# Threshold attention and a SwiGLU block on one core: the first nested output product issued in two pieces, with the last group's fourth product between them

## The chip, the core and the metric

The kernel runs on one core of a Trainium2 chip. A core has TensorE (PE: matmuls, and beside them its weight loads, PEld), VectorE (DVE), ScalarE (ACT), GpSimd (POOL) and SyncE (SP), which here issues DMA transfers. The metric is device time in microseconds (us) of one execution; lower is better. Before the change three runs took 1370.97, 1372.1 and 1374.73 us; the median is 1372.1 us.

## The reference

Attention in which only scores near the row's maximum survive, then a gated feed-forward block on the result:

```python
scores = scale * q @ k.T                      # per batch (8) and head (8), 576 x 576, head size 64
thresh = max(scores) - tau
scores = where(scores >= thresh, scores, -1e9)
attn   = softmax(scores)                      # with 1e-9 added to the sum
x      = concat_heads(attn @ v)               # 4608 tokens x 512
g      = x @ w_gate                           # 512 x 1536
out    = (g * sigmoid(g) * (x @ w_val)) @ w_out   # 1536 x 512
```

All numbers are float32.

## The kernel before

**Blocks.** The tokens are worked off in blocks 0 to 8. Blocks 0 to 7 hold the first 512 tokens of a batch each, as two halves t = 0, 1 of 256 tokens; block 8 holds the remaining 64 tokens of all batches. While the attention of one batch runs, the feed-forward part of the block before it is woven in. One block takes 12 slots of the attention loop; a slot (`slot_scores`, line 1705; `slot_rest`) is one set of score matmuls (tile names `sc`), their row maxima on VectorE, exponentials on ScalarE (line 1751), masking on VectorE (line 1753), scaling (line 1779 on ScalarE, line 1776 on POOL) and transposes (line 1781). In every third slot `attend` (line 1802, tiles `xa`) multiplies finished attention rows with v. It takes two PSUM banks, and ScalarE copies its result out (lines 1813, 1814).

**Gates and values.** The first feed-forward product and the value product of a block are made in six groups g (class `Group`), each with seven smaller matmul products instead of eight: p1 to p7, all through `mul` (line 993, tiles `pa`, `pb`, `pe`). The fourth product, `p4` (line 1073), adds the last part to bank `pb`. Its method `finish` (line 1041) then has ScalarE take the tanh of the gate (line 1045), VectorE multiply it with the bank's content (line 1046, output in `hall`), and POOL multiply by the halved gate (line 846). p4 needs the copy that ScalarE makes of the bank after p7 (line 1068). `gates_and_values` issues p4 of a group after p1 of the next one; for the last group there is no next one, and `end_gates` issues it from the output part.

**Output products.** For blocks 2 to 8 class `Deep` (line 1399) makes the product with `w_out` from seven half-size products, as a block matrix with two by two parts: a11, a12 (first half of the tokens), a21, a22 (second half), and sums of them. Five of the seven operands are split once more: `nested` (line 1462) issues seven sub-products of three 128 x 128 x 128 matmuls each (line 1473, tiles `px`), into two PSUM banks. Their operands come from `inner_sums` (line 1446): four sums j3, j1, j2, j4 of quarters of the operand, each 384 wide, on POOL in blocks 2 to 6 and on VectorE in the last two. The order of the sub-products in a nested product is

```python
ORDER = 0, 1, 3, 6, 4, 5, 2
```

where 0, 1 and 3 read quarters of the operand as it is, and 6, 4, 5 and 2 read the sums j3, j1, j2 and j4. Two of the seven operands stay whole (`flat`, line 1482, tiles `py`).

The steps of a block of `Deep` are, in blocks 2 to 6: `p1` (first nested product, operand a11, then ScalarE's copies of its two banks, lines 1495 and 1496), `gates_end` (the last group's p4, then `late`), `p2` (second nested product, operand a12, added in the same banks), `p5` (flat), `p6` (nested), `p3` (flat), `p7` and `p4` (nested). `p1` and `gates_end` come in slot 9 of the block, `p2` and `p5` in slot 10, `p6` and `p3` in slot 11, `p7` and `p4` in slots 0 and 1 of the next. Slot 10 begins with `attend` and the next scores, so between `gates_end` and `p2` TensorE runs xa and sc.

`late` (line 1431) plans the sums for the second product into the place of a11, so they wait for the first product, which reads a11:

```python
self.inner_sums(1, self.a12, self.a11, self.ready["a12"], self.m1, *j3)
```

then the sums a21 + a22 and a22 - s3, and last the sums of the operand of `p6` in the place where the sums for the first product were.

**Order.** A planner (`Plan`, line 31) runs along TensorE's order as it is written. For every job of another engine it keeps an estimated duration, the jobs it depends on and a rank; it issues the open jobs of each engine by estimated start and rank. An engine then executes its instructions in the order in which they were issued.

Of the kernel before, what the change touches and what calls it, by code (L numbers as in the profile page):

```python
# [27 lines left out]
class Plan:  # L28
# [68 lines left out]
    def pe(self, took, fn, *deps):  # L97
        self.force(*deps)
        for d in deps:
            if d is not None:  # L100
                self.t = max(self.t, (d.end if isinstance(d, Job) else d) + self.HOP)
        self.run(self.t)
        fn()
        self.t += took
        return self.t + self.PIPE
# [7 lines left out]
def kernel(  # L113
# [32 lines left out]
    NF2, DM2 = NF // 2, DM // 2  # L146
# [35 lines left out]
    NQ = 7  # L182
# [343 lines left out]
    def attend_tile(copy=lambda xa, fn: (fn(), give_back(xa))):  # L526
        if not unattended:
            return
        if not xts:
            for u, lo in enumerate((0, 2 * XW)):  # L530
                xts["full", u] = xall[:, lo:lo + XW].rearrange("p (c n) -> p c n", c=NCC)
            xts["last", 0] = xlast
        seg, t, pT, pT2 = unattended.popleft()
        vr, vr2 = seg["v"]
        n = pT2.shape[1]
        xa = bank("xa")
        for kt in range(KT):
            for h in range(2):
                nc.tensor.matmul(xa[h * D:(h + 1) * D, 0:n], vr[:, h, kt, :], pT[:, h, kt, :],
                                 start=(kt == 0), stop=False)  # L540
        nc.tensor.matmul(xa[:, 0:n], vr2, pT2, start=False, stop=True)
        u, lo = divmod(t * P, TC)
        to = xts[("last", 0) if t == NT else ("full", u)][:, seg["i"], lo:lo + n]
        copy(xa, lambda: nc.scalar.copy(to, xa[:, 0:n]))
# [155 lines left out]
    for n, seg in enumerate(segs[:2 * NP]):  # L700
# [3 lines left out]
        for x, t in enumerate(seg["tiles"]):  # L704
# [47 lines left out]
            if later and (n == NP or n == NP - 1 and x == 0):  # L752
                to, fr = later.popleft()
# [218 lines left out]
    tail = [False]  # L972
    MM = 0.4325
    gated = {}

    class Group:
# [25 lines left out]
        def p1(self, early=True):  # L1002
            self.a = take("pa")
            self.m1 = self.mul(self.a, self.w[0], x_block(self.c, 0, 0), True, *self.w_deps[0], *self.a.deps, *ready_x[self.c][0])
            self.a.bank.full = True
            if early:
                self.take_b()
# [10 lines left out]
        def p2(self):  # L1018
            u, self.u1_old = turn_of(u_bufs)
            self.u1_buf = u  # L1020
            if self.b is None:
                self.s1 = job("ACT", 0.55, lambda: nc.scalar.copy(u.ap, self.a.rows()), self.m1, *self.u1_old, rank=0)
                self.u1_old = []
            m = self.mul(self.a, self.w[1], x_block(self.c, 0, 1), False, *self.w_deps[1], self.cb if self.b else self.s1)
            self.m2 = m
# [70 lines left out]
    def four_sums(places, a11, a12, a21, a22, *deps):  # L1096

        p1, p2, p3, p4 = places
        j1 = job("DVE", 0.36, dve_tt(p1, a21, a22, ALU.add), *deps, rank=1)
        j2 = job("DVE", 0.36, dve_tt(p2, p1, a11, ALU.subtract), j1, rank=1)  # L1100
        j4 = job("DVE", 0.36, dve_tt(p4, a12, p2, ALU.subtract), j2, rank=1)
        return [j4, job("DVE", 0.36, dve_tt(p3, a11, a21, ALU.subtract), j4, rank=1)]
# [42 lines left out]
    class LateGroup(Group):  # L1145
        def nested(self, o, first, *deps):
            begun = set() if first else {0, 1}
            sums, wd = late_sums[self.c, self.g]
            ready, xd = x_deep[self.c]

            def fn():
                for n in ORDER:
                    b_, at_ = AT[n]
                    nc.tensor.matmul(self.es[b_].ap()[:, at_ * P:(at_ + 1) * P], wd[o][n], xd[o][n], start=b_ not in begun, stop=True,  # L1154
                                     skip_group_check=True)
                    begun.add(b_)

            return pe(NQ * MM / 2, fn, *deps, *sums, *ready)
# [231 lines left out]
    def weights_of(o):  # L1390
        b11, t3, b21, b22 = quarters(operands[o])
        return (b11, b21, b22, deeper_part(o, 2), deeper_part(o, 0), deeper_part(o, 1), t3)
# [3 lines left out]
    CW = NQ * P  # L1396
    spaces = tall[:, 0:CW], tall[:, CW:2 * CW], vall[:, NJ * D:NJ * D + CW]

    class Deep:


# [28 lines left out]

        def late(self, mark):
            c, n = self.c, NF2 // 2
            self.ready["a12"] = [gated[c, 0, n + x] for x in range(n)]
            self.ready["a22"] = [gated[c, 1, n + x] for x in range(n)]
            j3 = self.ready["s3"]
            self.inner_sums(1, self.a12, self.a11, self.ready["a12"], self.m1, *j3)
            self.ready["s1"].append(self.sum(self.a21, self.a21, self.a22, ALU.add, n - 1, j3[n - 1], gated[c, 1, NF2 - 1], rank=1))
            self.ready["s2"] = [self.sum(self.s2, self.a22, self.s3, ALU.subtract, x, j3[x], gated[c, 1, n + x], mark, rank=1) for x in range(n)]
            self.inner_sums(5, self.s2, self.place, self.ready["s2"], self.m1)

        def sum(self, out, a, b, op, x, *deps, rank=2):
            fs = slice(2 * x, 2 * x + 2)
# [16 lines left out]
        ORDER = 0, 1, 3, 6, 4, 5, 2  # L1459
        AT = {0: (0, 0), 1: (0, 1), 5: (0, 2), 2: (0, 3), 3: (1, 0), 4: (1, 1), 6: (1, 2)}  # L1460

        def nested(self, o, holds, first, *deps):

            ws = weights_of(o)
            begun = set() if first else {0, 1}
            for n in self.ORDER:
                a, ready = self.inner[o][n]
                bank_, at_ = self.AT[n]

                def fn(n=n, a=a, bank_=bank_, at_=at_):  # L1470
                    ps = holds[bank_].ap()[:, at_ * P:(at_ + 1) * P]
                    for f in range(NF2 // 2):
                        nc.tensor.matmul(ps, a[:, f, :], ws[n][:, f, :], start=bank_ not in begun, stop=True, skip_group_check=True)  # L1473
                        begun.add(bank_)

                m = pe(0.67, fn, *ready, *deps, *deep_jobs[o])
            return m
# [76 lines left out]

        def p1(self):
            self.x, deps = self.pair("px")
            self.m1 = self.nested(0, self.x, True, *deps)
            self.c1 = self.copies(self.spaces[0], self.x, self.m1, *u_list[0].jobs, *u_list[1].jobs)

        def gates_end(self):  # L1560
            end_gates()
            self.late(plan.t + plan.PIPE)

        def p2(self):
            m = self.nested(1, self.x, False, *self.c1)
# [322 lines left out]
    def end_gates():  # L1888
        state.pop("last_product")()
# [64 lines left out]
    for s, (n, x) in enumerate((n, x) for n in range(len(halved)) for x in range(NU3)):  # L1954
# [13 lines left out]
        elif s == 1:  # L1968
            box = []
            m = pe(1.0, lambda: attend_tile(lambda *y: box.extend(y)))  # L1970
# [93 lines left out]
```

## Time and profile before

| what | us |
|---|---|
| median of three runs | 1372.1 |
| lowest, highest run | 1370.97, 1374.73 |
| span of the profiled execution | 1369.2 |
| median run less that span | 2.9 |
| TensorE matmuls busy | 1351.0 |
| VectorE, ScalarE, POOL busy | 1070.9, 875.5, 719.9 |

The profile is of one execution, taken apart from the three runs. Its own time is its span, from the first to the last instruction, and what lies around it; the page gives no separate run time for it, so the distance to the median of the runs is shown instead. Times in the views are us from the span's start. In the chain of waits a row is start, length, engine, tile, line and how many records; each matmul appears as two records. `LNNN` is a line of the kernel.

### The profile page before, as it was taken

How to read it: one execution, taken by the hardware profiler on the slowest of the kernel's cores; microseconds unless marked ns; L12 is line 12 of the kernel's file. 1: busy time of each engine (PE TensorE's matmuls, PEld its weight loads, DVE VectorE, ACT ScalarE, POOL GpSimd, SP SyncE). 2: the span in 40 equal slices, each digit the busy share in tenths (PEclk: the TensorE clock that was granted, in tenths of full speed). 3: DMA queues.
4: the chain of work that ended last, by engine and by line, in shares of the span. 5: the costliest groups of instructions: out<-in, count | busy, mean ns of one | idle time of the engine just before them, and what ended most of it. 6: DMA issues, size and time to landing. Idle time of an engine off the chain costs nothing.

```text
span 1369.2 us, 39187 instructions
## 1 busy us (share of the span) xinstructions
PE 1351.0 (99%) x15590; PEld 1116.1 (82%) x15590; DVE 1070.9 (78%) x2815; ACT 875.5 (64%) x2277; POOL 719.9 (53%) x665
## 2 busy tenths in 40 slices
PE   8999999999999999999999999999999999999998
PEld 7777787778788788877887888877887788999998
DVE  7878888887887777777778777777777776787786
ACT  6888776666756766677776766776767764330330
POOL 2688598663564669434973387427943593000000
PEclk9999999999999999999999999999999999999999
DMA  8752424545525540654154513553165403524411
GB/s 177 200 185 90 82 60 133 146 121 156 151 52 155 144 98 27 181 159 117 37 171 128 150 36 128 144 144 87 36 192 144 113 19 143 162 78 146 151 66 32
DMA packets 208294, 162.32 MB, mean 119 GB/s; under 512 B 166128, under 2 KB 180464, under 8 KB 202736
## 3 DMA queue, kind: packets, MB, share of 16 engines
q1 hardware_dynamic: 203920, 158.86, 41.3%
q8 instruction: 124, 2.03, 0.6%
q10 hardware_dynamic: 4192, 0.95, 0.3%
q14 instruction: 58, 0.48, 0.1%
HBM read 138.28 MB, written 21.50 MB: 117 GB/s over the span
## 4 chain that ended last, share of the span: by engine, by line
PE 90%; DVE 3%; DMA 2%; POOL 2%; SPq 1%; issue 1%; ACT 1%; ACTq 0%; DVEq 0%; POOLq 0%
PE pb L993 18%; PE pa L993 12%; PE px L1473 12%; PE sc L1705 10%; PE pe L993 9%; PE xa L1802 9%; PE po L1269 5%; PE py L1482 5%; PE sc L1154 2%; PE pg L1200 2%; PE pv L1200 2%; PE pe L1154 1%; SPq L367 1%; DMA wo<-in_moe_w_val_dram 1%; PE sc L1473 1%
## 5 line engine op out<-in xcount | busy, mean ns | idle before, releaser
L1753 DVE SCALAR_TENSOR_TENSOR pall<-sc,th,pall 128x288 f32<-128x288 f32 x504 | 244.0, 514 | 65.1 <-ACT pall L1751 50.7
L993 PE MATMUL pb<-xall,big 128*128 128x256 f32 x1152 | 273.5, 380 | 0.0
L1751 ACT ACTIVATE pall<-sc,nm 128x288 f32<-128x288 f32 x504 | 232.2, 498 | 34.1 <-DVE pall L1753 33.8
L993 PEld LDWEIGHTS pb<-xall,big 128*128 128x128 f32 x1152 | 216.4, 190 | 31.0 <-issue 2.2
L1781 DVE STREAM_TRANSPOSE pall<-pall 128x576 f32<-128x576 f32 x252 | 189.7, 765 | 58.2 <-ACT pall L1779 41.4
L1779 ACT ACTIVATE pall<-pall,ri 128x288 f32<-128x288 f32 x415 | 189.8, 529 | 26.3 <-DVE ri L1767 25.8
L846 POOL TENSOR_TENSOR hall<-hall,tmp 128x512 f32<-128x512 f32 x80 | 102.3, 1279 | 159.3 <-DVE hall L1046 141.9
L993 PE MATMUL pa<-xall,big 128*128 128x256 f32 x768 | 183.4, 382 | 0.0
L993 PEld LDWEIGHTS pa<-xall,big 128*128 128x128 f32 x768 | 143.0, 190 | 22.2 <-issue 2.7
L1705 PE MATMUL sc<-kT,qT 64*32 64x144 f32 (+1 forms) x5376 | 150.0, 345 | 2.9 <-DVE pall L1753 1.7
L1726 DVE TENSOR_REDUCE mx<-sc 128x2 f32<-128x576 f32 x168 | 124.8, 743 | 28.6 <-PE sc L1705 28.1
L1705 PEld LDWEIGHTS sc<-kT,qT 64*32 64x32 f32 x5376 | 97.8, 106 | 56.9 <-issue 21.0
L993 PE MATMUL pe<-xall,big 128*128 128x256 f32 x576 | 137.2, 381 | 0.4 <-issue 0.4
L1802 PE MATMUL xa<-pall,vall 64*32 64x288 f32 x4032 | 133.0, 404 | 0.9 <-DVE hall L1046 0.8
L1776 POOL TENSOR_SCALAR pall<-pall,ri 128x288 f32<-128x288 f32 x89 | 88.9, 1010 | 67.0 <-DVE ri L1767 63.8
L993 PEld LDWEIGHTS pe<-xall,big 128*128 128x128 f32 x576 | 108.5, 190 | 17.3 <-issue 2.8
L1802 PEld LDWEIGHTS xa<-pall,vall 64*32 64x32 f32 x4032 | 76.5, 107 | 50.6 <-issue 7.4
L1761 ACT COPY sums<-sums 32x6 f32<-32x6 f32 x336 | 66.8, 199 | 45.6 <-DVE pall L1753 41.1
L1045 ACT ACTIVATE vall<-tmp 128x512 f32<-128x512 f32 x96 | 60.2, 630 | 24.6 <-DVE tmp L1058 9.0
L1482 PE MATMUL py<-wo,hall 128*128 128x256 f32 x336 | 74.8, 379 | 0.0
L1728 DVE TENSOR_REDUCE mx<-sc 128x1 f32<-128x288 f32 x168 | 74.8, 445 | 0.0
L846 POOL TENSOR_TENSOR tmp<-tmp 128x512 f32<-128x512 f32 x36 | 45.9, 1276 | 53.4 <-ACT tmp L1068 53.4
(258 smaller groups left out, 2481.3 us busy)
## 6 DMA issues: line engine op xcount, KB each, us to landing
big<-sums_hbm SPq DMA_DIRECT2D x42, 1024.0 KB, 5.4
big<-sums_hbm SPq DMA_DIRECT2D x48, 768.0 KB, 4.7
vall<-in_v_dram SPq DMA_DIRECT2D x112, 144.0 KB, 3.0
out_dram<-big SPq DMA_DIRECT2D x32, 256.0 KB, 3.0
qT<-in_q_dram SPq DMA_DIRECT2D x112, 72.0 KB, 4.8
kT<-in_k_dram SPq DMA_DIRECT2D x112, 72.0 KB, 3.0
wo<-in_moe_w_gate_dram SPq DMA_DIRECT2D x16, 384.0 KB, 4.1
wo<-in_moe_w_val_dram SPq DMA_DIRECT2D x16, 384.0 KB, 4.8
```

The lines of the kernel that those rows point to most:

```text
L846: return lambda: nc.gpsimd.tensor_tensor(out=out, in0=a, in1=b, op=op)
L993: nc.tensor.matmul(ps[:, i], w[:, k_, i * P:(i + 1) * P], x[:, k_, :], start=first and i == k_ == 0, stop=True, skip_group_check=True)
L1473: nc.tensor.matmul(ps, a[:, f, :], ws[n][:, f, :], start=bank_ not in begun, stop=True, skip_group_check=True)
L1482: nc.tensor.matmul(ps(), a[:, f, i * P:(i + 1) * P], operands[o][:, f, :], start=first and f == 0, stop=True, skip_group_check=True)
L1705: nc.tensor.matmul(pss[h][(slice(g * G, (g + 1) * G), *part)], qT[hs, col:col + G], kT[hs, c * SH + keys[0]:c * SH + keys[1]], start=True, ...
L1726: rs.append(job("DVE", 0.72, lambda n=n, tile_=tile_: nc.vector.tensor_reduce(out=mx[:, n:n + 2, 0], in_=tile_[:, :, 0:SH], axis=AX.X, op= ...
L1751: ej = job("ACT", 0.42, lambda x=x, n=n: nc.scalar.activation(ps[x], scs[x], AF.Exp, bias=nm[:, n:n + 1]), ej, *((masks[h, 0], masks[h, 1] ...
L1753: masks[x] = job("DVE", 0.45, lambda x=x, n=n: nc.vector.scalar_tensor_tensor(out=ps[x], in0=scs[x], scalar=th[:, n:n + 1], in1=ps[x], op0 ...
L1776: scaled.append(job("POOL", 1.02, lambda x=x, n=n: nc.gpsimd.tensor_scalar(out=x, in0=x, scalar1=ri[:, n:n + 1], scalar2=None, op0=ALU.mul ...
L1779: scaled.append(job("ACT", 0.46, lambda x=x, n=n: nc.scalar.activation(x, x, AF.Copy, scale=ri[:, n:n + 1]), rj, rank=rank))
L1781: seg["turned"].append(job("DVE", 0.72, lambda both=both: nc.vector.transpose(out=both, in_=both), *scaled, rank=rank))
L1802: nc.tensor.matmul(holds[a].ap()[x * G:(x + 1) * G, 0:SH].rearrange("d (i q) -> d i q", q=G), vr[rs, h, j, ds], p[rs, h, :, j, :], start=( ...
```

## The change

The first nested product is issued in two pieces in blocks 2 to 6. `p1` issues its first three sub-products (0, 1, 3) and plans the sums for the second product, which now depend on those three. `gates_end` issues the last group's fourth product, then the other sums as before, then the remaining four sub-products (6, 4, 5, 2) and the copies of the banks, and then plans the sums for `p6`, which depend on the whole product as before. Blocks 7 and 8 (`tail[0]` true) keep the order of before through the other branch.

```diff
+    AHEAD = 3
...
         def late(self, mark):
             c, n = self.c, NF2 // 2
-            self.ready["a12"] = [gated[c, 0, n + x] for x in range(n)]
             self.ready["a22"] = [gated[c, 1, n + x] for x in range(n)]
             j3 = self.ready["s3"]
-            self.inner_sums(1, self.a12, self.a11, self.ready["a12"], self.m1, *j3)
             self.ready["s1"].append(...)
             self.ready["s2"] = [...]
-            self.inner_sums(5, self.s2, self.place, self.ready["s2"], self.m1)
...
-        def nested(self, o, holds, first, *deps):
+        def nested(self, o, holds, first, *deps, lo=0, to=NQ):
 
             ws = weights_of(o)
-            begun = set() if first else {0, 1}
-            for n in self.ORDER:
+            begun = {self.AT[n][0] for n in self.ORDER[:lo]} if first else {0, 1}
+            for n in self.ORDER[lo:to]:
...
         def p1(self):
             self.x, deps = self.pair("px")
-            self.m1 = self.nested(0, self.x, True, *deps)
+            self.ready["a12"] = [gated[self.c, 0, NF2 // 2 + x] for x in range(NF2 // 2)]
+            if tail[0]:
+                self.first_product(*deps)
+            else:
+                self.second_sums(self.nested(0, self.x, True, *deps, to=AHEAD))
+
+        def first_product(self, *deps, lo=0):
+            self.m1 = self.nested(0, self.x, True, *deps, lo=lo)
             self.c1 = self.copies(self.spaces[0], self.x, self.m1, *u_list[0].jobs, *u_list[1].jobs)
+
+        def second_sums(self, m):
+            self.inner_sums(1, self.a12, self.a11, self.ready["a12"], m, *self.ready["s3"])
 
         def gates_end(self):
             end_gates()
+            if tail[0]:
+                self.second_sums(self.m1)
             self.late(plan.t + plan.PIPE)
+            if not tail[0]:
+                self.first_product(lo=AHEAD)
+            self.inner_sums(5, self.s2, self.place, self.ready["s2"], self.m1)
```

## The prediction

> **What bounds the kernel now.** I read the shares and the clock first, then the chain of work that ended last, then TensorE's waits, and then the five places where those waits fall. From the page:
>
> ```profile
> PE 1351.0 (99%) x15590; PEld 1116.1 (82%) x15590; DVE 1070.9 (78%) x2815; ACT 875.5 (64%) x2277; POOL 719.9 (53%) x665
> ...
> PEclk9999999999999999999999999999999999999999
> ...
> PE 90%; DVE 3%; DMA 2%; POOL 2%; SPq 1%; issue 1%; ACT 1%; ACTq 0%; DVEq 0%; POOLq 0%
> ```
>
> TensorE is busy for 99% of the span at its full granted clock. So a change of order gains only where TensorE stands still, and loses where it makes TensorE stand. The waits after 345 us (TensorE's matmuls, then its weight loads; us in total, times, longest) show what there is to win:
>
> ```profile
> PE xa L1802 <- DVE hall L1046: 0.8, 5, 0.2
> ...
> PEld xa L1802 <- DVE hall L1046: 3.5, 5, 0.7
> ```
>
> Five times, once in each of blocks 2 to 6, the attend step (xa) waits for VectorE's multiply at line 1046: 0.70 us of the weight loads each time. The matmul row says only 0.16, because 8 matmul records of xa still run and their ends are modelled. So I take the price from the chain, in order of time (start, us, what). First block 2 at the wait, then the same steps where nothing waits:
>
> ```profile
> 517.87 4.88 PE px L1473 x42
> 522.76 1.74 PE pb L993 x8
> 524.50 0.02 issue
> 524.52 0.70 DVE hall L1046
> 525.22 0.04 issue
> 525.26 4.33 PE xa L1802 x132
> 529.59 0.21 PE sc L1705 x4
> 529.80 0.03 PE xa L1802 x4
> 529.83 1.50 PE sc L1705 x50
> 531.33 4.97 PE px L1473 x42
> ...
> 554.84 4.89 PE px L1473 x42
> 559.72 4.53 PE xa L1802 x144
> 564.25 1.50 PE sc L1705 x63
> ```
>
> The fourth product (pb) ends at 524.50. VectorE multiplies it out of its bank, and only then can xa use that bank. The stretches from the first nested product (px) to the second, in all five blocks (length, then busy time by engine):
>
> ```profile
> 517.87:531.33 13.46, 13.30 (x260) 10.25 (x259) 9.08 (x25) 9.73 (x30) 13.30 (x13) 1.00 0.05 14
> 666.18:679.64 13.46, 13.30 (x259) 10.25 (x259) 9.08 (x25) 9.72 (x30) 13.30 (x13) 1.00 0.07 19
> 813.02:826.47 13.45, 13.29 (x259) 10.22 (x259) 9.08 (x25) 9.72 (x30) 13.29 (x13) 1.00 0.05 13
> 960.24:973.69 13.45, 13.29 (x259) 10.24 (x259) 9.08 (x25) 9.72 (x30) 13.29 (x13) 1.00 0.07 18
> 1107.09:1120.55 13.46, 13.30 (x260) 10.25 (x259) 8.39 (x24) 9.73 (x30) 13.30 (x13) 1.00 0.06 17
> ```
>
> The fifth busy number is POOL's: it works nearly without a pause there, so its order matters.
>
> **The change part by part.** The built order of TensorE differs from before in five places only, one per block 2 to 6: four matmuls of pb now stand after the third of the seven px sub-products. Blocks 7 and 8 take the other branch and keep their order. Matmul counts stay equal.
>
> *1. The wait of xa.* Undisturbed, the stretch is 4.88 (px after scores) + 1.73 (pb) + 4.53 (xa) + 1.50 (sc) = 12.64 us. The five stretches sum to 67.28, five undisturbed ones to 63.20: the wait costs 4.08 us. Does it go? A px without scores ahead takes 4.69 (row at 1142.41), so a sub-product is 0.67 and the start after scores adds 0.19. In block 2 the first three end at 517.87 + 0.19 + 2.01 = 520.07, pb ends at 521.81, the other four at 524.49. On VectorE the multiply now stands right after the maxima's reduction (ends 521.54) and ahead of all six masks, so it would run 521.83 to 522.53 (0.69 by its row). Its tanh on ScalarE (0.63) stands behind scalings that end at 519.01 and needs POOL's sum of 518.01 to 519.29: done near 519.9. The bank is free 2.0 us before xa wants it. Next latest for xa are the transposes of the score tiles, which end at 521.49, 3.0 us before. Bounds: 0 (another release takes the place) to 4.08; I take 4.08, because a margin of 2.0 stands against rows that agree within 0.02 across blocks.
>
> *2. The last sub-product of the second product.* It reads the fourth of its input sums on POOL, which runs 534.31 to 535.26, behind four token sums; so the second product takes 4.97, 4.95, 4.97, 4.97 and 4.96 against 4.88: 0.42 us. In the new order two of the four sums start once the first three sub-products are done, and the fourth stands ahead of the token sums. Laid out with POOL's own durations from 519.24 (one 384-wide sum 1.0, two more 1.96, then 1.25, the gate multiply 1.25, 1.25, 0.98, 1.25, 1.25, 1.0) it ends near 530.4. The sub-product needs it at 530.52 + 0.19 + 4.02 = 534.7. Bounds 0 to 0.42; I take 0.42.
>
> *3. The moved fourth product.* Its steps: four matmuls, ScalarE's tanh, VectorE's multiply, POOL's gate multiply; as the last group of the block it issues no load. It waits for ScalarE's copy of 516.30 to 516.88 and would start at 520.07: 3.2 us of cover (5.9 before). The split makes one more pair of boundaries between px and pb, both 128-row shapes. Rows: pb after px 1.74 against 1.73, and px after pb at 1334.70 follows in 1.73. So 0 to 0.02 per block; I take 0.
>
> The Trainium skill ("TensorE: Matmul & The Clock Gate", "Single matmul latency" and "Back-to-back issue gap") gives a lone matmul a constant of about 166 ns that a stream hides. If each new boundary broke the stream, that would be an estimated 0.8 us against the change in all. The 1.73 rows show no such break where pb and px meet without a wait.
>
> *4. What is queued behind moved work.* VectorE: the first mask slips from 522.30 to about 522.53, hidden, since the multiply no longer stands between later masks. ScalarE: the copies of the first product now stand behind five exponentials instead of two and wait until 524.49; 0.58 and 0.50 put their end near 525.6, the sixth exponential (0.50) near 526.1, its mask (0.52) near 526.6. The next scores want the score banks at 529.02, the second product wants the copies at 530.52. Cost 0, cover 2.4 and 4.9 us. If the cover is gone, every further us costs one, five times. POOL: the sums for the fifth operand still wait for all seven sub-products and end near 538.4, their product starts near 542.2. The last sum of the seventh operand slips past the a12 update to about 545.8, its product starts near 554. VectorE: a q transpose moves ahead of the totals and may wait for POOL's scaling to about 540.1; the scalings behind it have until the next but one scores. SP's queue keeps its order, no transfer is added; loads issued from px and py start with them, some 0.9 us earlier per block.
>
> *Sum.* 4.08 + 0.42 - 0 = 4.5 us. The profiled span becomes 1369.2 - 4.5 = 1364.7. The median of the runs shown, 1372.1, stands 2.9 us above that span (start, end and the spread of runs); I keep those 2.9: 1372.1 - 4.5 = 1367.6. That is 0.33%, a little past the 0.3% (4.1 us) that a measurement of this kernel can tell from no change.
>
> **The rivals.**
>
> *A. The wait only shrinks, or a later release takes it back.* For it: DMA engines are 95% busy in the product stretch at 554.84, and VectorE 9 of 13.5 us in the stretch at 517.87. Against it: after 345 us TensorE waits for nothing else but two issue pieces of 0.5 and 0.4, and loads move with the matmuls that release them. If half of part 1 stays: 1372.1 - 2.0 - 0.4 = 1369.7.
>
> *B. The change does not do what it says.* The dependence on the first piece is worth only part 2 (0.42); the gain comes from the place of pb. If VectorE still reaches the multiply as late as the second piece ends, as it would if the tanh stayed at its 522.17 behind an exponential and the masks went first, the wait stays: 1372.1 - 0.4 = 1371.7. Against it: the built orders of ScalarE and VectorE have both moved up.
>
> *C. Slower: ScalarE's queue.* The first product's copies hold up the sixth exponential, its mask, and so the next scores. It begins to cost when the sixth mask ends 2.4 us later than my 526.6; it eats the gain of 0.9 per block at 3.3 us, and makes the kernel over 0.3% slower at 3.3 + 0.8 = 4.1 us (mask after 530.7). Time there: 1372.1 + 4.1 = 1376.2. Against it: the copies need only the matmul end at 524.49, and no row delays that by 4 us.
>
> **How the numbers follow.** Forecast 0.78, A 0.10, B 0.06, C 0.06. The forecast's own range is 1366.3 to 1369.5: the sum, less the 1.1 that the lowest run lies under its median, and up to 1.9 for part of the 2.6 above it. About 0.79 of the forecast falls under 1368.0 (0.3%): 0.78 x 0.79 = 0.62 faster. The rest of it with A and B gives 0.32 the same; C gives 0.06. The range takes in A and most of B: 1365.8 to 1371.5. Most left out is C, and part of the forecast's low side.
>
> **What would show it.** Right: no waits of xa for line 1046; the five stretches near 12.65; second products at 4.88; pb between two px pieces, 2.2 and 2.7 us long; a span near 1364.7. Wrong: a wait of sc for the masks (C), of xa for line 1046 (B), a px or pb longer by 0.1 or more (the boundary), or new waits at the first groups of the next block for loads (A).

## The result

The changed kernel takes 1368.13 us (median of 7 runs, 1366.24 to 1371.92), the kernel before 1373.27 us beside it (7 runs, 1370.97 to 1374.73). The ratio is estimated at 0.9969 (the medians alone give 0.9963), with a 95% interval of 0.9958 to 0.998: 0.31% less, just past what a measurement of this kernel can tell from no change. The forecast was 1367.6 us.

### The profile after

The page of the changed kernel's profiled execution has the same picture as before:

```profile
PE 1350.8 (99%) x15590; PEld 1120.1 (82%) x15590; DVE 1069.4 (78%) x2815; ACT 876.6 (64%) x2277; POOL 717.6 (52%) x665
...
PEclk9999999999999999999999999999999999999999
```

The waits of TensorE's matmuls after 345 us (us in total, times, longest) no longer name line 1046, and the row of xa's weight loads for that line, 3.5 us before, is gone too. A wait in block 7 is new: a nested product that is written to the scores' banks (sc, line 1472) waits for VectorE at line 849.

```profile
PE sc L1719 <- issue: 1.2, 2, 0.7
PE sc L1472 <- DVE pall L849: 0.5, 1, 0.5
PE px L1472 <- issue: 0.4, 1, 0.4
```

The chain of waits of the changed kernel in block 2, in order of time (start, us, what). All of it stands 4.24 us later than before, for a reason that comes below.

```profile
520.46 1.65 PE sc L1719 x64
522.11 2.21 PE px L1472 x18
524.31 1.73 PE pb L993 x8
526.04 2.68 PE px L1472 x24
528.72 4.53 PE xa L1816 x144
533.25 1.50 PE sc L1719 x62
534.74 4.88 PE px L1472 x42
539.63 5.18 PE py L1481 x24
```

TensorE runs from the scores to py without a piece of any other engine. The fourth product stands between two pieces of the first nested product, 2.21 and 2.68 us long; together they are 4.89, where the undivided one took 4.88. The attend step takes its undisturbed 4.53. The stretches from the first nested product to the second, first and last of five, in the view by windows (length, then busy time of TensorE's matmuls, its weight loads, VectorE, ScalarE and POOL, then the granted clock, the DMA share and GB/s):

```profile
522.11:534.74 12.63, 12.63 (x259) 10.17 (x259) 9.07 (x25) 9.56 (x29) 12.63 (x13) 1.00 0.05 13
...
1107.80:1120.44 12.64, 12.64 (x260) 10.17 (x259) 8.39 (x24) 9.57 (x29) 12.64 (x13) 1.00 0.04 11
```

The five sum to 63.17 us against 67.28: 4.11 less. The second products, each taken from the end of the scores ahead of it to its own end as in the chain's rows, sum to 24.41 against 24.82: 0.41 less.

### Why the two profiled spans do not show it

The span of this execution is 1369.8 us, 0.6 longer than before's 1369.2. Split at the first scores of the woven part, in the view by windows, before and then after (columns as above):

```profile
0.00:153.06 153.06, 141.62 (x1144) 110.87 (x1145) 123.46 (x263) 126.31 (x268) 100.95 (x75) 1.00 0.62 160
153.06:1369.20 1216.14, 1209.41 (x14446) 1005.24 (x14446) 947.40 (x2553) 749.24 (x2010) 618.98 (x590) 1.00 0.40 113
```

```profile
0.00:157.25 157.25, 145.21 (x1145) 113.42 (x1145) 123.22 (x263) 126.32 (x268) 100.09 (x75) 0.98 0.59 156
157.25:1369.80 1212.55, 1205.58 (x14446) 1006.68 (x14446) 946.20 (x2553) 750.29 (x2010) 617.52 (x590) 1.00 0.40 114
```

The first stage, which the change doesn't touch, took 4.19 us longer in this execution; everything behind it took 3.59 less. This execution's own time was 1371.92, the longest of the seven, and 2.1 above its span. Among executions whose mean clock was 1.000, the kernel before ran at 1370.48 (median of 13) and the changed one at 1366.76 (median of 4), both from the comparison of the changed kernel again below: 3.7 us, as the second row says.

Of the 4.5 us gained in blocks 2 to 6, some is given back. In the chain of waits of the changed kernel, block 7 hangs on a load:

```profile
1205.42 5.79 DMA big<-sums_hbm
...
1211.24 0.44 DVE pall L849
...
1227.26 2.27 PE sc L1472 x18
```

In the kernel before, the chain at the same place is TensorE alone:

```profile
1225.65 1.34 PE px L1473 x12
1226.98 2.01 PE sc L1473 x18
```

The last weight load of block 7 (768 KB) landed 5.8 us after its issue, before 4.6 us; VectorE's sums of weights slip, and the product that reads them waits 0.5 us. Pieces that the profile calls issue come to 1.6 us after and 0.9 before. So -4.5 + 0.5 + 0.7 = -3.3, against the -3.59 of the windows; the last 0.3 the trace doesn't resolve.

### The profile page after: what moved, and what is told of

Same layout as the page of the kernel before. It is cut to its first block, busy times and chain, and to the rows that moved or that the text cites. A ratio compares the mean times of both kernels' runs of the same rounds, so it can differ in the third digit from the quotient of the medians.

```text
span 1369.8 us, 39206 instructions
## 1 busy us (share of the span) xinstructions
PE 1350.8 (99%) x15590; PEld 1120.1 (82%) x15590; DVE 1069.4 (78%) x2815; ACT 876.6 (64%) x2277; POOL 717.6 (52%) x665
## 4 chain that ended last, share of the span: by engine, by line
PE 89%; DVE 4%; DMA 2%; POOL 2%; issue 1%; SPq 1%; ACT 1%; ACTq 0%; DVEq 0%; POOLq 0%
PE pb L993 18%; PE pa L993 12%; PE px L1472 12%; PE sc L1719 10%; PE xa L1816 9%; PE pe L993 9%; PE po L1269 5%; PE py L1481 5%; PE pg L1200 2%; PE pv L1200 2%; PE sc L1154 2%; SPq L367 1%; DMA vall<-in_v_dram 1%; PE pe L1154 1%; PE sc L438 1%
## 5 line engine op out<-in xcount | busy, mean ns | idle before, releaser
L1719 PE MATMUL sc<-kT,qT 64*32 64x288 f32 (+1 forms) x5376 | 147.4, 345 | 3.0 <-DVE pall L1767 1.4
L1816 PE MATMUL xa<-pall,vall 64*32 64x288 f32 x4032 | 129.0, 404 | 0.1
```

The lines of the kernel that those rows point to most:

```text
L1719: nc.tensor.matmul(pss[h][(slice(g * G, (g + 1) * G), *part)], qT[hs, col:col + G], kT[hs, c * SH + keys[0]:c * SH + keys[1]], start=True, ...
L1816: nc.tensor.matmul(holds[a].ap()[x * G:(x + 1) * G, 0:SH].rearrange("d (i q) -> d i q", q=G), vr[rs, h, j, ds], p[rs, h, :, j, :], start=( ...
```

## The experiments

The theory is the prediction's: moving pb frees the bank that xa wants (step 1), and early sums free the second product (step 2). The rivals are B, by which the sums' dependence on the first piece is worth 0.42 us and no more, and C, by which the copies on ScalarE hold up the sixth mask. "Stretch" is the length from the first nested product to the second in one of blocks 2 to 6; it is 13.46 before and 12.63 after. "Rest" is the time from the first scores of the woven part to the end, 1216.14 and 1212.55.

### The changed kernel again

No edit.

> The changed kernel once more, to see what of its first profile comes back. Theory (bank release): the five stretches from the first to the second nested product last 12.63 to 12.65 us, the second products 4.88, and from the first scores of the woven part to the end the execution is 4.5 us shorter than before, less the 0.5 to 0.6 us that block 7 lost in the first profile to a late load, if that comes back. Rival (the difference is run spread in the first 150 us): the time from those first scores to the end is the same as before, 1216 us.

1369.03 us (median of 12) against 1371.54 for the kernel before: ratio 0.9974, interval 0.9961 to 0.9987. One of the 12 took 3555 us and has no trace; it is not explained, and without it the median is 1368.86. The stretches are 12.63 again, the second products sum to 24.41, the rest is 1212.78, and block 7 waits 0.6 us at the same place. What the first profile showed is the kernel, and not that execution.

### The kernel before again

> The kernel before once more, for a second trace. Both theories of the change: the five stretches of 13.46 us come back. For block 7: if the last weight load lands in under 5 us here too, its slowness belongs to the kernels with the moved fourth product; if it takes 5.5 us or more, it is chance.

1373.43 us (one run). The stretches are 13.46 again, with the same wait for line 1046 (0.8 us in five times by the matmuls), the rest is 1215.95, and block 7's load lands in 4.4 us without a wait. From this pair the gain of the rest is 3.2 us.

### pb behind the whole product, sums early

```diff
                 self.second_sums(self.nested(0, self.x, True, *deps, to=AHEAD))
+                self.first_product(lo=AHEAD)
...
         def gates_end(self):
             end_gates()
...
-            if not tail[0]:
-                self.first_product(lo=AHEAD)
```

> Only the dependence of the sums changes (three sub-products instead of seven); the fourth product stays behind the whole first product. Bank release theory: the stretches stay at 13.46 us with xa waiting for line 1046 five times, the second products shorten from 4.96 to 4.88, in all 0.4 us faster than before, not to be told from no change by the clock. Rival (the gain of the change comes from the sums): stretches near 12.64, 4.5 us faster.

1371.74 us (median of 12): ratio 1.0004 to the kernel before, interval 0.9992 to 1.0016. Stretches 13.46. In the view of waits, the old wait is there unchanged:

```profile
PE xa L1815 <- DVE hall L1046: 0.8, 5, 0.2
```

The second products sum to 24.43, 0.4 less than before. The rest is 1214.90, 1.2 less than before; the other 0.8 lies outside these steps and is not explained, so a difference of the rest by less than 1 us is not to be put down to a step. Early sums alone give step 2 and nothing of step 1: the wait of xa belongs to the place of pb.

### pb moved, sums late

```diff
-                self.second_sums(self.nested(0, self.x, True, *deps, to=AHEAD))
+                self.nested(0, self.x, True, *deps, to=AHEAD)
...
             if not tail[0]:
                 self.first_product(lo=AHEAD)
+                self.second_sums(self.m1)
```

> Only the place of the fourth product changes (after three sub-products); the sums of the second product wait for the whole first product, as before. Theory A (the gain is the bank release alone, the earlier sums are worth 0.42 us): stretches of 12.64 us and second products near 4.96, in all 4.1 us faster than before. Theory B (the earlier sums are needed once the fourth product is moved): in the issued order of POOL the third and fourth of these sums now stand behind the four token sums and two sums of other operands; laid out with POOL's durations the fourth ends near 537.4 in block 2's times of before, the second product then ends near 538.2 instead of 535.4: stretches of 12.64 but second products near 7.7 us, in all 4.1 - 14 = 10 us slower than before.

1389.04 us (median of 4): ratio 1.0125, interval 1.0107 to 1.0144, 17.5 us slower than the kernel before, where 10 had been expected. The stretches are 12.63, so step 1's gain is there in full. But the second product now waits for POOL's sums (view of waits):

```profile
PE px L1472 <- POOL hall L846: 11.3, 10, 1.3
```

The five second products take 40.38 us against 24.82: 15.56 us lost, 7.7 to 8.4 us each where 7.7 had been expected. In block 2, POOL (line 846) works without a pause from 519.07 us on, the gate multiplies and the token sums among it, and the last sum that the second product needs runs from 538.48 to 539.49, behind them. In the times of before it ends at 537.19 (this block starts 2.30 us later here); in the changed kernel it ended at 530.27. Stretches and second products account for 15.56 - 4.11 = 11.45 us; the rest of this kernel is 1232.65, 16.5 more than before. The next rows show where most of the other 5 us are. The chain of waits up to the first two py of block 2:

```profile
538.48 1.01 POOL hall L846
539.49 0.04 issue
539.54 1.24 PE px L1472 x6
540.78 6.56 PE py L1481 x24
...
553.87 5.18 PE py L1481 x24
```

The same in the view by windows of this kernel (the granted clock is the third number from the end):

```profile
538.00:540.00 2.00, 1.02 (x9) 0.83 (x9) 1.74 (x9) 1.60 (x4) 2.00 (x3) 1.00 0.00 0
540.00:542.00 2.00, 2.00 (x9) 1.73 (x8) 1.04 (x6) 1.41 (x6) 1.92 (x3) 0.50 0.01 4
542.00:544.00 2.00, 2.00 (x8) 1.65 (x7) 1.93 (x5) 2.00 (x6) 2.00 (x2) 0.64 0.00 0
544.00:546.00 2.00, 2.00 (x11) 1.77 (x10) 1.93 (x3) 1.24 (x3) 2.00 (x3) 1.00 0.38 131
```

After the two waits the granted clock is 0.50 from 540.0 to 543.4, and py takes 6.56 us in place of 5.18. It takes 6.59, 6.02 and 5.97 in three of the other four blocks, 5.18 in one: 4.4 us in all. So 11.45 + 4.4 = 15.9 of the 16.5 us are named: a stall of TensorE cost not only its own length, and this part had not been expected.

What follows for rival B: its first half, that the gain comes from pb's place, is what these two runs show. Its second half, that the dependence on the first piece is worth 0.42, is not: with pb moved, the kernel without that dependence is 20 us slower than with it, 4.4 us of it through the clock. The two parts of the change are not terms to be added. The edit also plans these sums after those of `late`, so the run does not part the dependence itself from the place that the sums then take on POOL.

### pb ahead of the whole product

```diff
             else:
+                end_gates()
                 self.second_sums(self.nested(0, self.x, True, *deps, to=AHEAD))
+                self.first_product(lo=AHEAD)
...
         def gates_end(self):
-            end_gates()
             if tail[0]:
+                end_gates()
                 self.second_sums(self.m1)
             self.late(plan.t + plan.PIPE)
-            if not tail[0]:
-                self.first_product(lo=AHEAD)
```

> The fourth product stands ahead of the whole, undivided first product; the sums wait for three sub-products. Bank release theory: any earlier place will do, stretches of 12.64 us, no wait for line 1046. In the issued order of POOL the fourth sum of the second product stands behind the token sums and one more, near 535.3 in block 2's times of before against a need at 534.7: second products near 5.5 us, in all 4.1 - 2.9 = 1.2 us faster than before. Rival (the split of the first product is what helps): stretches stay near 13.4.

1371.98 us (median of 12): ratio 1.0002, interval 0.9991 to 1.0013. No wait for line 1046 is left, and pb with the whole product, xa and scores takes as long as in the changed kernel: step 1 again in full, 4.1 us. But the second products take 5.65 each, 28.28 in sum against 24.82, 3.5 us more. The chain of waits of block 2 shows POOL's last sum ending just ahead of the last sub-product:

```profile
534.82 0.96 POOL hall L846
535.78 0.04 issue
535.83 0.94 PE px L1472 x6
```

The fourth sum again stands behind the token sums on POOL and ends when it did before: 535.78 less 0.61, the later start of this block, is 535.17, against 535.26. But the last sub-product now wants it 0.8 us earlier, so POOL becomes the limit of the second product. That pb's gate multiply, which now runs ahead of these sums, is what keeps the fourth one behind the token sums is argued and not shown. I had expected 1.2 us of gain; the rest is 1215.90, 0.2 less than before. So three places of pb give three releases: behind the product VectorE's multiply is late, ahead of it POOL's sums are late, between the pieces neither.

### pb after six sub-products

```diff
-    AHEAD = 3
+    AHEAD, PB_AT = 3, 6
...
                 self.second_sums(self.nested(0, self.x, True, *deps, to=AHEAD))
+                self.nested(0, self.x, True, *deps, lo=AHEAD, to=PB_AT)
...
             if not tail[0]:
-                self.first_product(lo=AHEAD)
+                self.first_product(lo=PB_AT)
```

> The changed kernel with the fourth product behind six of the seven sub-products instead of three; the sums still wait for three. Bank release theory: only the time at which VectorE has emptied the bank counts. pb ends 0.7 us before xa may start and VectorE takes it behind three masks, so the bank is free near 0.2 us after xa's turn: stretches of 12.8 to 12.9 us against 12.63 (three ahead) and 13.46 (none behind), a short wait for line 1046 again, second products 4.88. In all about 3.3 us faster than before. Rival (any split does it): stretches of 12.63.

1368.5 us (median of 7): ratio 0.9969 to the kernel before, interval 0.9957 to 0.9981, as good as the changed kernel. The chain of waits of block 2:

```profile
520.20 4.21 PE px L1472 x36
524.42 1.73 PE pb L993 x8
526.15 0.67 PE px L1472 x6
526.82 4.68 PE xa L1817 x144
531.50 1.49 PE sc L1720 x59
532.99 4.89 PE px L1472 x42
```

The attend step takes 4.68 in place of 4.53, the stretch 12.79: one sub-product of 0.67 behind pb covers all but 0.15 of the 0.83 us that the wait costs in a block. The views of waits name no wait for line 1046 here, although a short one had been expected; VectorE's multiply ends at 526.87, 0.05 us after xa's turn, so that the 0.15 is this wait is argued. This sizes the margin of step 1. Five times 0.15 is lost to the changed kernel; block 7's load landed in 4.4 us here, without the wait of 0.5.

### The first product's copies six times

```diff
-            self.c1 = self.copies(self.spaces[0], self.x, self.m1, *u_list[0].jobs, *u_list[1].jobs)
+            for _ in range(1 if tail[0] else 6):
+                self.c1 = self.copies(self.spaces[0], self.x, self.m1, *u_list[0].jobs, *u_list[1].jobs)
```

> The changed kernel, but ScalarE copies the first product's two banks six times over into the same place in blocks 2 to 6: five extra pairs of 0.85 us, 4.25 us, stand ahead of the sixth exponential. It prices the slower rival of the prediction (the copies hold up exponential, mask and next scores). In the changed kernel the sixth mask ends 2.57 us before the scores start. Theory (cover of 2.57, then one for one): scores wait about 1.7 us in each of five blocks, 8.4 us slower than the changed kernel, 4 slower than before. Rival without cover: 4.25 a block, 21 us slower than the changed kernel. Rival with more cover: no difference.

The copies repeat the same data in the changed kernel's order. 1379.03 us (median of 5): ratio 1.0052 to the kernel before, interval 1.0039 to 1.0066. The scores now wait for the masks, in the view of waits and in the chain:

```profile
PE sc L1720 <- DVE pall L1768: 7.1, 5, 1.4
```

```profile
529.64 0.49 ACT tmp L1494
530.13 0.38 ACT tmp L1495
530.51 0.41 ACT pall L1766
...
530.94 0.54 DVE pall L1768 x2
...
531.52 1.70 PE sc L1720 x48
```

This is rival C's road: copies, sixth exponential, sixth mask, scores. Five more pairs of 0.49 + 0.38 put 4.35 us on ScalarE, and the stretch grew by 14.69 - 12.63 = 2.06 (1.7 had been expected). The chain has no gap between these steps, so beyond the cover each us should cost one; then 2.3 us are covered, where the prediction had 2.4. This is one point, and no second number of copies was run. C's mechanism is real, and the change stands some 2.3 us away from it.

### Block 8's row loads in the other order

The changed kernel's 768 KB load of block 7 lands late, and two loads of rows for block 8 stand beside it on SP's queue.

```diff
-            for kh in range(2):
+            for kh in (1, 0):
                 src = last_hbm[:, 2 * kh:2 * kh + 2, :].rearrange("p c (t n) -> p t c n", t=2)
```

> The changed kernel, with the two loads of block 8's rows into the free half of the place issued behind the two that wait for block 7's products, so that they no longer follow block 7's last weight load at once on the same queue. Theory (these 0.5 MB slow the weight load to 5.6 to 5.9 us, and VectorE's sums and the wait of 0.3 to 0.6 us in block 7 follow from it): the load lands in about 4 us, VectorE waits less than 0.5 us for it, no wait of the nested product of block 7 for VectorE, from the first scores of the woven part to the end 0.5 us less than in the changed kernel (1212.0 to 1212.2). Rival (the load is slow for another reason, or chance): it still lands in 4.5 to 6 us.

1367.17 us (median of 5): ratio 0.9961, interval 0.9947 to 0.9974, which overlaps that of the changed kernel. The load still landed in 5.7 us, the product still waited 0.4 us, and the rest is 1212.80. The order of the row loads is not the cause.

What the traces show beside it: one transfer of the instruction queue (one packet, 0.02 MB in the view of DMA queues) in this neighbourhood. Before, it comes between 1210.7 and 1211.2 us, when the load of 1205.6 has landed; after, between 1207.7 and 1208.2, in the middle of the load of 1205.42. In all ten profiles the load took 4.4 to 4.6 us where this transfer came behind it (the kernel before, both times; sums early; pb after six) and 5.3 to 5.9 where it fell into it (the changed kernel, both times; pb moved and sums late; pb first; copies six times; rows in the other order). The two go together in all ten profiles, but that is not a cause shown: no run moved the transfer alone. It stays open.

## Why the prediction was right

*Step 1, the wait of xa (4.08 us).* Measured 4.11 by the five stretches. The prediction's laid-out times also hold. From the changed kernel's timeline in block 2, VectorE's multiply, POOL's fourth sum, ScalarE's second copy and VectorE's sixth mask (less 4.24 us they are in the prediction's times):

```profile
526.08 0.69 DVE L1046 SCALAR_TENSOR_TENSOR hall<-vall,pb 128x512 f32<-128x512 f32 x1 [0.31 <-PE pb L993]
...
533.50 1.01 POOL L846 TENSOR_TENSOR hall<-hall 128x384 f32<-128x384 f32 x1
...
529.24 0.49 ACT L1495 COPY tmp<-px 128x384 f32<-128x384 f32 x1
...
530.16 0.52 DVE L1767 SCALAR_TENSOR_TENSOR pall<-sc,th,pall 128x288 f32<-128x288 f32 x1
```

The multiply starts at 521.84, where 521.83 was written. It waited only for pb itself, so nothing on VectorE's queue stood in its way, and rival B's "multiply as late as before" did not come. pb ahead of all seven sub-products, after three and after six show the release from three sides.

*Step 2, the second product's last sub-product (0.42).* Measured 0.41. POOL's fourth sum ends at 534.51 - 4.24 = 530.27, where 530.4 was written, and 0.4 of it comes without step 1 in the run with early sums and pb last.

*Step 3, the extra boundary (0).* The two pieces and pb take 2.21 + 1.73 + 2.68 = 6.62 us, the undivided product and pb 4.88 + 1.74. The estimate that the prediction drew from the Trainium skill ("TensorE: Matmul & The Clock Gate", "Single matmul latency") for broken streams, 0.8 us, is not what happens where pb and px follow without a wait.

*Step 4, the covers.* The sixth mask ends at 530.68 - 4.24 = 526.44 (526.6 was written), the copies at 525.49 (525.6). The cover of 2.4 us is 2.3 by the run with copies six times. VectorE did wait for POOL's q scaling, 1.07 us, as the prediction said it might, and nothing behind it came late.

*What the sum lacked.* Three things, on either side of what I looked at. Block 7 gives back 0.5 to 0.6 us through a load that lands late; rival A named loads, but only at the first groups of the next block. Pieces that the profile calls issue, 0.7 us more than before in this pair, make up the rest. And the 2.9 us between span and median were taken as one constant: own times stand 2.1 to 2.2 us above their spans in every run that has both numbers, and the other 0.8 is spread between executions; the first stage alone took 153.1 to 157.3 us in the ten profiles, a spread as large as the gain. The rest's gain of 3.6 us is thus what the change is worth in this pair of profiles, 0.9 less than the sum (3.2 in the second pair).

*What was luck.* The median, 1368.13, came within 0.6 us of the forecast's 1367.6, closer than the sum deserves. The forecast started from 1372.1 for the kernel before, whose seven runs beside the changed kernel then had a median of 1373.27; these medians differ by 5.1 us, those of the next comparison (1371.54 and 1369.03) by 2.5. The low end of the forecast's own range also holds a slip: 1367.6 less 1.1 is 1366.5, where 1366.3 was written.

*What was wrong in a rival.* B put the dependence of the second product's sums on the first piece at 0.42 us, which is its worth with pb in the old place (0.4 measured). With pb in the new place, dependence and place in POOL's order together are worth some 20 us. The prediction laid out POOL's queue for the new order only; had it laid out pb moved with late sums, it would have seen the sums behind the whole product's.

## What to carry to other kernels

When one engine is busy for 99%, lay out every queue behind a moved step in absolute times, from the rows before, and compare each end with the moment it is wanted: here all four such times held within 0.2 us. Two parts of one change can each look small or even harmful alone and be worth more together, since a step moved ahead pushes others back on a third engine's queue; price them in both orders. And a gain of a few us should be read between two landmarks that enclose the change, since an untouched stage can differ by as much from one execution to the next.

## What the runs showed of the hardware

*Two waits of TensorE close together were followed by half its clock.* With pb moved and sums late, TensorE's matmuls stood still for 1.27 and then 0.98 us, with 0.93 us of matmuls between, and in four of five blocks the granted clock then fell to 0.50 (block 2 is shown above). Block 3 has the same two waits and kept its clock; the row behind them, in the view by windows:

```profile
692.00:694.00 2.00, 2.00 (x11) 1.77 (x10) 1.10 (x4) 1.76 (x7) 1.92 (x3) 1.00 0.00 0
```

By this profile's clock records the four falls begin at 540.02, 840.39, 990.58 and 1140.77 us and last 3.41 us each, and the distances between them are whole multiples of 3.413 us. Cut the span into stretches of that length with these times among the borders: in the one just ahead of each fall, TensorE's matmuls idle for 1.95 to 2.08 us. In block 3 a border at 690.21 us parts the waits, and the stretches on its two sides hold 1.34 and 0.92 us. So the same waits may cost clock or not by where they fall; this is read from one execution, and no run moved the waits against the borders. Single waits did not lower the clock: 0.16 us in each block of the kernel before and 1.42 us in each block with copies six times (both by the matmuls), all at clock 1.00. The Trainium skill ("TensorE: Matmul & The Clock Gate", "Part 1: The HAM clock gate") puts a return to half clock after an idle window of about 3.4 us, and as long to come back. The 3.4 us at half clock agree; ahead of them about 2 us of idle time were enough, and not in one piece, so a full idle window is not needed.

*A fall of the clock goes with the spread of the first stage.* In the changed kernel's first profile, TensorE idles around 39 us in the first stage, and the granted clock falls behind it (view by windows):

```profile
38.00:40.00 2.00, 0.60 (x7) 0.24 (x5) 2.00 (x3) 1.78 (x6) 1.41 (x2) 1.00 0.62 78
40.00:42.00 2.00, 0.90 (x3) 0.78 (x5) 1.93 (x7) 1.25 (x4) 1.70 (x1) 0.75 0.91 325
42.00:44.00 2.00, 2.00 (x7) 1.12 (x6) 1.15 (x3) 0.79 (x2) 0.11 (x1) 0.50 1.03 382
44.00:46.00 2.00, 2.00 (x18) 1.65 (x17) 1.83 (x3) 2.00 (x6) 1.81 (x2) 0.50 1.20 260
```

From 40 to 50 us the clock was 0.66 in this execution, 0.66 and 0.83 in others of the changed order, and 1.00 in both profiles of the kernel before and in those of sums early, pb first and pb after six. TensorE idles there in all of them, and how long doesn't decide: it was busy for 0.55 of the 2 us from 38 to 40 in the run with pb after six, without a fall, and for 1.39 in the second profile of the changed kernel, with one. Runs of the kernel before have mean clocks from 0.996 to 1.000 too. So the fall comes in some executions and not in others, and in the changed kernel's first profile it goes with a first stage 4.2 us longer, part of which is the idle time itself. What decides when it comes there, no run here shows.
